# Loading the query weights as fifteen strided 16-row transfers, one of them ahead of the first keys

## The chip, the cores and the metric

The kernel runs on one core of a Trainium2 chip. A time is the device time of one execution in microseconds (us); the median of several executions is quoted.

## The reference, cut to what matters

One decode step: four batch entries, one token each, width 512. The token is normalised, multiplied by the query weights `wq` (512 x 4096), scored against 1024 cached keys for 8 key heads, and the result goes through `wo`; an MLP gate runs beside it.

```python
xn = layernorm(x)
q  = (xn @ wq).reshape(B, 1, 32, 128)          # wq: 512 x 4096 bf16, 4 MB
p  = softmax(q @ K[:, :, -1024:] / sqrt(128))  # K: 8 MB read
s  = (p @ V[:, :, -1024:]) @ wo                # V: 8 MB, wo: 4 MB
g  = silu(mlp(layernorm(xn)))                  # w1, w2: 3.7 MB
out = x + s * g
```

The kernel reads 28.85 MB and does little arithmetic on it.

## The kernel before

All large loads are issued by SyncE (SP), one after the other, and run on the core's 16 DMA engines. The order is K0, K1, wq in two halves, K2 to K7, then V (with the two MLP weights behind V0 and V1) and `wo`. Row `4p + c` of `wq` goes to partition `p`, slot `c`, so each partition's 32 KB are contiguous in memory.

```python
    def load_k(g):
        d_k[g] = pg.dma("sp", "k%d" % g, lambda e: e.dma_start(
            kv_buf[:, g, :, :].rearrange("p c d -> p (c d)"), cache_rows(A_k_cache, g)))
    # ... (cut)
    load_k(0)
    load_k(1)
    wq_r = A_wq.rearrange("(p c) n -> p c n", c=4)
    d_wq = [pg.dma("sp", "wq%d" % c, lambda e, c=c: e.dma_start(
        wq_sb[:, 2 * c:2 * c + 2, :], wq_r[:, 2 * c:2 * c + 2, :])) for c in range(2)]
    for g in range(2, HKV):
        load_k(g)
    # ... (cut) the query product waits for the two halves of wq in turn
    add("pe", lambda pe: f_q(pe, 0), v_xT, d_wq[0])
    t_q = add("pe", lambda pe: f_q(pe, 1), d_wq[1])
```

The softmax here doesn't subtract the row's maximum and nothing guards it: scores larger than these inputs give would overflow.

## Time and profile before

| | before |
|---|---|
| time, median | 77.41 us (77.17 to 78.25, 3 runs) |
| span of the profile | 75.4 us |
| first bytes of the large stream | 2.20 us |
| stream rate between 5 and 70 us | about 424 GB/s |
| 16 KB packet, median | 611 ns |
| last landing of `wq` | 19.5 us |
| end of the stream (last landing of `wo`) | 72.25 us |

A descriptor is one row's copy order. A "packet" is one copy's record in the trace; a "landing" is one rise of the semaphore of a transfer after its issue: a K transfer has 16 of them, the 4-row x transfer 4. Both are counted in the trace one by one; it doesn't say which DMA engine one belongs to. The strip, the windows, the chain and the queue's timeline of this kernel are shown and read in the prediction below.

One line more, from the timeline of the last matmuls: start, length, what, and in brackets the idle time ahead of it and what ended that.

```profile
68.61 3.42 PE L486 MATMUL psM<-OW,wo_sb 128*128 128x4 bf16 x120 [0.51 <-DVE OW L472]
72.29 0.37 PE L486 MATMUL psM<-OW,wo_sb 128*128 128x4 bf16 x8 [0.26 <-DMA wo_sb<-in_A_wo_dram]
```

The last eight matmuls waited 0.26 us for the end of the stream.

### The profile page before, as it was taken

The page shows a single profiled execution, that of the slowest core. Times are in us where ns is not written, and L with a number is a line of the kernel's source. Part 1 is how long each engine was busy: PE and PEld are TensorE (multiplying, and loading weights), DVE is VectorE, ACT ScalarE, POOL GpSimd, SP SyncE. Part 2 cuts the span into 40 slices and gives each one's busy share as a digit, 9 for nine tenths or more (in the row PEclk, how much of TensorE's full clock was granted, in tenths as well). Part 3 has the DMA queues.
Part 4 walks back from the last instruction along what each step waited for, and adds up shares of the span by engine and source line. Part 5 has one row for each costly group of instructions (what it writes and reads, how often), then busy time and mean ns, then how long its engine had stood idle before and what let it go on. Part 6 is the DMA issues. An engine that isn't in the chain of part 4 may idle for free.

```text
span 75.4 us, 2408 instructions
## 1 busy us (share of the span) xinstructions
PE 54.1 (72%) x1107; PEld 46.0 (61%) x1107; DVE 38.0 (50%) x84; ACT 9.0 (12%) x16; POOL 4.5 (6%) x13
## 2 busy tenths in 40 slices
PE   0009992500659999999999945999759989937950
PEld 0009871200228999999999935999459766806930
DVE  0878996000033599999999000000891678781010
ACT  0611000000054031231131520000200000000000
POOL 6970000000000000000000000000000000000000
PEclk9999999955555799999999997555555555555555
DMA  0899999999999999999999999999999999999600
GB/s 2 280 413 439 454 426 417 434 434 382 434 421 421 421 430 430 443 413 437 451 389 439 440 412 396 426 430 426 434 417 421 419 411 424 417 408 412 255 13 2
DMA packets 4213, 28.99 MB, mean 384 GB/s; under 512 B 486, under 2 KB 491, under 8 KB 1644
## 3 DMA queue, kind: packets, MB, share of 16 engines
q1 hardware_dynamic: 4160, 28.84, 91.7%
q8 instruction: 8, 0.13, 0.6%
q10 hardware_dynamic: 44, 0.01, 0.1%
q14 instruction: 1, 0.01, 0.0%
HBM read 28.85 MB, written 0.00 MB: 382 GB/s over the span
## 4 chain that ended last, share of the span: by engine, by line
DMA 46%; PE 29%; SPq 20%; DVE 2%; issue 1%
DMA wo_sb<-in_A_wo_dram 24%; DMA wq_sb<-in_A_wq_dram 22%; SPq L454 17%; PE psK L279 16%; PE psS L298 6%; PE psO L362 3%; PE psS L294 2%; SPq L207 2%; PE psK L374 1%; DVE q_sb L368 1%; SPq L219 1%; PE psS L516 1%; PE psM L486 1%; SPq L212 0%; DVE o_bf L518 0%
## 5 line engine op out<-in xcount | busy, mean ns | idle before, releaser
L279 PE MATMUL psK<-ident,kv_buf 128*128 128x128 bf16 x256 | 21.0, 234 | 5.7 <-DMA kv_buf<-in_A_k_cache_dram 5.7
L285 DVE COPY kt_buf<-psK 128x1024 bf16<-128x1024 bf16 x32 | 20.7, 686 | 2.2 <-PE psK L279 2.2
L279 PEld LDWEIGHTS psK<-ident,kv_buf 128*128 128x128 bf16 x256 | 16.5, 105 | 6.3 <-DMA kv_buf<-in_A_k_cache_dram 5.7
L298 PE MATMUL psS<-qT,kt_buf 128*128 128x16 bf16 x256 | 10.3, 170 | 0.0
L298 PEld LDWEIGHTS psS<-qT,kt_buf 128*128 128x128 bf16 x256 | 9.6, 97 | 1.1 <-issue 0.3
L316 PEld LDWEIGHTS psO<-P_buf,kv_buf 128*128 128x128 bf16 x256 | 7.7, 103 | 2.2 <-issue 1.9
L316 PE MATMUL psO<-P_buf,kv_buf 128*128 128x16 bf16 x256 | 8.2, 174 | 0.3
L392 PE MATMUL psM<-yT,w_sb 128*128 128x4 bf16 x56 | 5.7, 204 | 1.8 <-issue 1.8
L362 PE MATMUL psO<-wq_sb,xT 128*32 128x512 bf16 x32 | 2.9, 503 | 5.6 <-DMA wq_sb<-in_A_wq_dram 5.6
L306 ACT ACTIVATE P_buf<-psS 128x512 bf16<-128x512 f32 x8 | 4.8, 598 | 15.6 <-PE psS L298 15.6
L329 DVE TENSOR_REDUCE den_sb<-psS 128x16 f32<-128x512 f32 x8 | 5.5, 689 | 1.7 <-PE psS L322 1.4
L400 DVE TENSOR_SCALAR t_sb<-u_sb 128x56 f32<-128x56 f32 x1 | 0.2, 192 | 11.4 <-ACT u_sb L399 11.4
L392 PEld LDWEIGHTS psM<-yT,w_sb 128*128 128x128 bf16 x56 | 4.5, 153 | 2.2 <-issue 2.1
L362 PEld LDWEIGHTS psO<-wq_sb,xT 128*32 128x32 bf16 x32 | 0.8, 112 | 6.9 <-DMA wq_sb<-in_A_wq_dram 5.7
L368 DVE CAST q_sb<-psO 128x512 bf16<-128x512 f32 x1 | 0.7, 691 | 8.4 <-PE psO L362 8.4
L322 PE MATMUL psS<-P_buf,ones_bf 128*128 128x512 bf16 x8 | 4.5, 561 | 0.0
L486 PE MATMUL psM<-OW,wo_sb 128*128 128x4 bf16 x128 | 3.8, 166 | 0.8 <-DVE OW L472 0.5
L486 PEld LDWEIGHTS psM<-OW,wo_sb 128*128 128x128 bf16 x128 | 3.6, 104 | 0.9 <-issue 0.6
L294 PE MATMUL psS<-negm,ind 128*128 128x512 bf16 x8 | 3.3, 410 | 0.0
L419 PE MATMUL psM<-hT,w_sb 128*128 128x4 bf16 x56 | 2.1, 167 | 1.4 <-DVE hT L411 1.4
L394 PE MATMUL psM<-ones_bf,b_sb 1*128 1x4 bf16 x14 | 3.0, 215 | 0.0
L419 PEld LDWEIGHTS psM<-hT,w_sb 128*128 128x128 bf16 x56 | 1.8, 105 | 1.9 <-DVE hT L411 1.9
(63 smaller groups left out, 28.9 us busy)
## 6 DMA issues: line engine op xcount, KB each, us to landing
kv_buf<-in_A_k_cache_dram SPq DMA_DIRECT2D x8, 1024.0 KB, 21.3
kv_buf<-in_A_v_cache_dram SPq DMA_DIRECT2D x8, 1024.0 KB, 22.6
wq_sb<-in_A_wq_dram SPq DMA_DIRECT2D x2, 2048.0 KB, 13.9
w_sb<-in_B_w_dram SPq DMA_DIRECT2D x2, 1792.0 KB, 31.2
wo_sb<-in_A_wo_dram SPq DMA_DIRECT2D x3, 1024.0 KB, 24.8
wo_sb<-in_A_wo_dram SPq DMA_DIRECT2D x1, 512.0 KB, 21.4
wo_sb<-in_A_wo_dram SPq DMA_DIRECT2D x2, 256.0 KB, 17.8
x<-in_A_x_dram ACTq DMA_DIRECT2D x2, 2.0 KB
```

Source lines behind the costliest of these rows:

```text
L279: last = pe.transpose(psK[n % NB][:, j * 128:(j + 1) * 128], kv_buf[:, g, u * UT + j, :], ident[:, :])
L285: cp[n] = add("dve", lambda e: e.tensor_copy(kt_buf[:, n % NKT, :], psK[n % NB][:, 0:1024]), t, sc.get(n - NKT))
L294: pe.matmul(psS[g % 2][:, 0:512], ind[:, :], negm[:, :], start=True, stop=False, skip_group_check=True)
L298: last = pe.matmul(psS[g % 2][:, c * 16:(c + 1) * 16], kt_buf[:, n % NKT, j * 128:(j + 1) * 128], qT[:, g * 16:(g + 1) * 16], start=False, ...
L306: ex[g] = add("act", lambda e: e.activation(P_buf[:, g, :], psS[g % 2][:, 0:512], AF.Exp, scale=SCALE), sc[n])
L316: last = pe.matmul(pso[:, 0:16], kv_buf[:, (HKV + g) % NS, c, :], P_buf[:, g, c * 16:(c + 1) * 16], start=(c == 0), stop=(c == NC - 1))
L322: den[g] = add("pe", lambda pe: pe.matmul(psS[g % 2][:, 0:512], ones_bf[:, :], P_buf[:, g, :], start=True, stop=True), ex[HKV - 2 + g % 2] ...
L329: v = add("dve", lambda e: e.tensor_reduce(den_sb[:, cs], bass.AP(psS[g % 2], 0, [[512, 128], [1, 16], [16, NC]]), AX.X, ALU.add), den[g])
L362: last = pe.matmul(psO[m // 4][32 * s:32 * s + 32, 0:512], xT[:, c, :], wq_sb[:, c, m * 512:(m + 1) * 512], start=(c == 0), stop=(c == 3), ...
L392: pe.matmul(o, bass.AP(w1_sb, c * F + k, [[4 * F, 128], [FC, 128]]), yT[:, c * 4:(c + 1) * 4], start=(c == 0), stop=False)
L454: e.dma_start(wo_sb[:, g0:g1, i0:i1, :], wo_r[:, g0:g1, i0:i1, :]))))
L486: last = pe.matmul(psM[:, PS_W + c * 4:PS_W + (c + 1) * 4], wo_sb[:, g, i, c * 128:(c + 1) * 128], OW[:, i, g * 4:(g + 1) * 4], start=firs ...
```

## The change

Its intent: let the first transfer have few descriptors, so that all 16 DMA engines get work sooner, and keep the partitions of the following ones in the same pattern. The group `s` of a transfer is every eighth partition, `s, 8+s, ..., 120+s`: sixteen rows.

```diff
+    wq_r = A_wq.rearrange("(q s c) n -> s q (c n)", s=8, c=4)
+    wq_v = wq_sb[:, :, :].rearrange("p c n -> p (c n)")
+    d_wq = [[pg.dma("sp", "wqa", lambda e: e.dma_start(wq_v[0:128:8, :], wq_r[0, :, :]))], []]
     load_k(0)
     load_k(1)
-    wq_r = A_wq.rearrange("(p c) n -> p c n", c=4)
-    d_wq = [pg.dma("sp", "wq%d" % c, lambda e, c=c: e.dma_start(
-        wq_sb[:, 2 * c:2 * c + 2, :], wq_r[:, 2 * c:2 * c + 2, :])) for c in range(2)]
+    for c in range(2):
+        for s in range(1, 8):
+            n = HQ * DH * 2
+            d_wq[c].append(pg.dma("sp", "wq%d_%d" % (c, s), lambda e, n=n, c=c, s=s: e.dma_start(
+                wq_v[s:128:8, c * n:(c + 1) * n], wq_r[s, :, c * n:(c + 1) * n])))
@@ (cut) the query product @@
-    add("pe", lambda pe: f_q(pe, 0), v_xT, d_wq[0])
-    t_q = add("pe", lambda pe: f_q(pe, 1), d_wq[1])
+    add("pe", lambda pe: f_q(pe, 0), v_xT, *d_wq[0])
+    t_q = add("pe", lambda pe: f_q(pe, 1), *d_wq[1])
```

## The prediction

Passages are cut from the text below, each marked. Two terms of the sum are +9.7 us and -1.0 us, the author's estimate: the packets of wq take twice as long as the 611 ns measured (16 x 0.611 = 9.8 us becomes 19.5), and about 1 us of that comes back where the group changes. The two sums: 85.8 us with these terms, 77.1 us without. Rivals: R1 (no loss, 77.1 us) and R2 (the loss shrinks to one group of three or four transfers, about 2 us: 79 us); the chances given were 0.60 for a doubling, 0.10 for a partial loss (R2, R3) and 0.30 for none.

> **What bounds the kernel now.** I read the strip of forty slices first, then the table of windows, then the chain of waits, then the DMA queue's own timeline. The strip (busy tenths of each engine, then the DMA's share and rate) says which resource never rests:
>
> ```profile
> PE   0009992500659999999999945999759989937950
> DVE  0878996000033599999999000000891678781010
> DMA  0899999999999999999999999999999999999600
> GB/s 2 280 413 439 454 426 417 434 434 382 434 421 421 421 430 430 443 413 437 451 389 439 440 412 396 426 430 426 434 417 421 419 411 424 417 408 412 255 13 2
> ```
>
> PE and DVE have holes; the DMA row stands at 9 from the third slice to the thirty-seventh. The windows (length, busy time of PE, PEld, DVE, ACT and POOL, granted clock, DMA share, GB/s) give the rate:
>
> ```profile
> 5.00:10.00 5.00, 4.26 (x48) 3.94 (x48) 4.59 (x12) 0.20 (x1) 0.34 (x1) 1.00 1.04 429
> 10.00:15.00 5.00, 2.74 (x42) 1.62 (x40) 2.63 (x6) 0.00 (x0) 0.00 (x0) 1.00 1.02 436
> ...
> 55.00:60.00 5.00, 4.47 (x125) 4.07 (x126) 2.73 (x9) 0.18 (x1) 0.00 (x0) 0.50 1.00 419
> ...
> 70.00:71.00 1.00, 1.00 (x44) 1.00 (x41) 0.00 (x0) 0.00 (x0) 0.00 (x0) 0.50 0.71 272
> 71.00:72.00 1.00, 1.00 (x36) 0.94 (x33) 0.00 (x0) 0.00 (x0) 0.00 (x0) 0.50 0.36 139
> ```
>
> So this is one stream of 28.85 MB at about 424 GB/s. 28.85 MB / 424 GB/s is 68.0 us; it starts a little after 2 us and its last bytes land at 72.25. The packets say the same per engine: 8 KB took 309 ns and 16 KB 611 ns, nearly always, which is 26.5 GB/s an engine, times 16 is 424. All 16 engines run flat out, so only three things can move the time: an earlier start of the stream, a lower rate in it, or a longer tail.
>
> The chain of waits (start, length, what) names other pieces, and must be read with that in mind:
>
> ```profile
> 2.78 16.73 DMA wq_sb<-in_A_wq_dram
> ...
> 41.55 0.60 SPq L454
> ...
> 54.36 17.89 DMA wo_sb<-in_A_wo_dram
> ```
>
> It goes through the query weights (landing at 19.5 us), the score phase and the output-weight issues. But while PE waited for wq the stream moved 410 to 436 GB/s of other data. Bringing wq in earlier therefore buys nothing by itself; wq's place matters only through the bytes of the stream. After 72.25 there are 3.2 us of tail (last eight matmuls, two DVE operations, output DMA), and the measured time stands 2.0 us above the profiled span (77.41 against 75.4). The change touches neither.
>
> The queue's timeline (start, length, line, issue) shows the beginning that the change aims at:
>
> ```profile
> 0.81 1.26 SPq L207 DMA_DIRECT2D kv_buf<-in_A_k_cache_dram  x2
> 2.12 1.17 SPq L219 DMA_DIRECT2D wq_sb<-in_A_wq_dram  x2
> 3.33 3.84 SPq L207 DMA_DIRECT2D kv_buf<-in_A_k_cache_dram  x6
> ```
>
> A 128-row transfer costs SP about 0.6 us to issue; the first K bytes move in the window from 2.00 to 2.25 us.
>
> [...]
>
> **The change, part by part.**
>
> *Removed:* two wq transfers of 128 descriptors of 16 KB, 1.17 us of SP issue. *Added:* one transfer of 16 descriptors of 32 KB, and fourteen of 16 descriptors of 16 KB. The bytes are equal: 4 MB, 256 KB an engine, 9.6 us of stream.
>
> *Issue.* The output DMA, also 16 rows, took SP 0.36 us. Fifteen of those are 5.4 us against 1.17, 4.2 us more of SP. Does SP starve the stream? Each small transfer carries 256 KB, 0.62 us of stream, for about 0.40 us of issue with its gap, and 2.5 MB (6 us) stand queued ahead of them. K2 is issued near 8 us instead of 3.3, V0 near 12 instead of 9.0; by then over 3 MB are queued. No cost.
>
> *Semaphore packets.* 13 transfers more, one 9 ns packet per engine each (the trace's 4-byte packets): 0.12 us on the stream.
>
> *Start.* The x transfer, issued at 0.80, moved its first bytes in the window from 1.50 to 1.75; K0, issued at 0.81 with 128 rows, in that from 2.00 to 2.25. A 16-row first transfer should follow x: about 0.45 us earlier. Its 32 KB an engine last at least 1.2 us, long enough for K0's descriptors to be there. Gain about 0.45 us, all of it on the path.
>
> [...]
>
> [...] 77.4 - 0.45 + 0.12 + 9.7 - 1.0 = 85.8 us. [...] 77.4 - 0.45 + 0.12 = 77.1 us.
>
> Would a wq that lands near 29 us instead of 19.5 bring another bound? V2 was issued at 26.96 after the scores began. 18.4 MB stood ahead of it in the stream, enough to about 45 us, so an issue near 36 us still comes in time. PE's work after the scores stays behind the stream as before.
>
> **The rivals.** [...] *R3: small transfers are paced by SP.* Each would need over 0.62 us of issue; 0.36 us speaks against it. It would cost under 3 us. *R4: the start gain is larger than I take it.* The stream can't begin before SP's first issue at 0.81 plus x's 0.8 us, so nothing beyond 0.7 us.
>
> **Range and chances.** [...] Over 2% faster means 1.55 us gained, three times what the earlier start offers: 0.03. Within 2%: 0.31. Slower by over 2%: 0.66. The predicted time lies in the larger heap, 85.4 us; an honest 8-in-10 range has to reach into the other: 76.8 to 87.0.
>
> **What would show it.** [...] between about 6 and 26 us the rate is 210 to 300 GB/s instead of 424, the DMA share stays near 1, and 16 KB packets of wq take about 1.2 us instead of 0.611; wq's last landing moves to 27 to 29 us; the end of the stream moves to about 81 us. [...] The start: first stream bytes at about 1.75 us. Issue: small transfers at 0.3 to 0.4 us on SP, no low DMA share between them. [...]

## The result, and the profile after

| | before | after |
|---|---|---|
| time, median | 77.45 us (6 runs) | 86.92 us (86.77 to 87.5, 6 runs) |
| span of the profile | 75.4 us | 85.1 us |
| first bytes of the stream | 2.20 us | 2.20 us |
| 16 KB packets of `wq`, median | 611 ns | 1253 ns |
| last landing of `wq` | 19.5 us | 27.9 us |
| end of the stream | 72.25 us | 81.94 us |

The ratio is 1.1216, 95% interval 1.1157 to 1.1274: 12% slower. (A ratio here is the mean time of one kernel's fast runs over that of the other's in the same rounds, so it isn't quite the ratio of the medians quoted.)

The strip of the changed kernel, the same two rows as before:

```profile
DMA  0999999999998999999999999999999999999810
GB/s 2 256 301 425 409 216 246 185 216 216 246 193 192 427 423 431 416 427 423 416 447 428 401 439 439 407 415 423 420 427 431 427 410 416 423 410 418 326 49 2
```

A slice is now 2.1 us. The DMA row is as full as before, but from the sixth slice to the thirteenth the engines move 185 to 246 GB/s. They are busy with half the bytes. The windows (columns as before; the last three are granted clock, DMA share and GB/s) date it:

```profile
5.00:8.00 3.00, 0.00 (x0) 0.00 (x0) 2.20 (x7) 0.20 (x1) 0.34 (x1) 1.00 0.96 394
10.00:25.00 15.00, 6.04 (x73) 4.20 (x71) 4.70 (x9) 0.00 (x0) 0.00 (x0) 0.78 1.02 220
```

(The view counts a packet whole in the window in which it starts. So a share can read above 1, and a short window can read far above 424 GB/s.) While K0 and K1 pass, the rate is 394; while the fourteen wq transfers pass, it is 220 at a DMA share of 1.02. The engines show a full busy share at half the usual 424 GB/s, since a 16 KB packet takes 1253 ns instead of 611; that is the sign to look for here. The queue's timeline (start, length, line, issue):

```profile
0.80 0.62 SPq L220 DMA_DIRECT2D wq_sb<-in_A_wq_dram  x1
1.48 1.26 SPq L207 DMA_DIRECT2D kv_buf<-in_A_k_cache_dram  x2
2.78 8.97 SPq L226 DMA_DIRECT2D wq_sb<-in_A_wq_dram  x14
11.80 3.83 SPq L207 DMA_DIRECT2D kv_buf<-in_A_k_cache_dram  x6
```

The opening transfer has 16 rows and still took SP 0.62 us, as a K transfer does; the fourteen took 0.64 us each with their gaps. The chain of waits still names wq, and is of as little help as before:

```profile
11.17 16.77 DMA wq_sb<-in_A_wq_dram
...
66.64 15.30 DMA wo_sb<-in_A_wo_dram
```

Where the 9.7 us of span went can be read from landings. K1's last landing moved from 8.41 to 11.07 us, 2.66 us later; 1.24 us of that is the opening transfer's own 512 KB at 424 GB/s, now ahead of K1, so 1.42 us is loss. From there to the last landing of wq it took 16.87 us for 3.67 MB; at the kernel before's pace (15 of its 16 landings had come by 18.11 us, from 8.41, for 4.19 MB) that would be 8.5 us: 8.4 us of loss. Together 9.8 us, against 9.69 us by which the end of the stream moved. That leaves nothing of size for the rest of the kernel.

### The profile page after: what moved, and what is told of

Its sections match the earlier page's. It is cut to its first block, busy times and chain, and to the rows that moved or that the text cites. A ratio compares the mean times of both kernels' runs of the same rounds, so it can differ in the third digit from the quotient of the medians.

```text
span 85.1 us, 2415 instructions
## 1 busy us (share of the span) xinstructions
PE 54.0 (63%) x1095; PEld 47.1 (55%) x1107; DVE 38.5 (45%) x84; ACT 9.0 (11%) x16; POOL 4.5 (5%) x13
## 4 chain that ended last, share of the span: by engine, by line
DMA 38%; SPq 30%; PE 26%; issue 2%; DVE 1%
DMA wq_sb<-in_A_wq_dram 20%; SPq L461 18%; DMA wo_sb<-in_A_wo_dram 18%; PE psK L286 15%; SPq L226 9%; PE psS L305 6%; PE psO L369 2%; SPq L207 1%; PE psK L381 1%; DVE q_sb L375 1%; SPq L220 1%; PE psS L523 0%; PE psM L493 0%; SPq L212 0%; DVE o_bf L525 0%
## 5 line engine op out<-in xcount | busy, mean ns | idle before, releaser
L286 PE MATMUL psK<-ident,kv_buf 128*128 128x128 bf16 x256 | 21.6, 239 | 8.2 <-DMA kv_buf<-in_A_k_cache_dram 8.2
L286 PEld LDWEIGHTS psK<-ident,kv_buf 128*128 128x128 bf16 x256 | 17.2, 108 | 8.5 <-DMA kv_buf<-in_A_k_cache_dram 8.2
L369 PE MATMUL psO<-wq_sb,xT 128*32 128x512 bf16 x32 | 3.8, 625 | 10.9 <-DMA wq_sb<-in_A_wq_dram 10.9
L376 ACT ACTIVATE q_sb<-psO 128x512 bf16<-128x512 f32 x1 | 0.6, 597 | 23.2 <-PE psO L369 23.2
```

What stands on the lines that cost most here:

```text
L286: last = pe.transpose(psK[n % NB][:, j * 128:(j + 1) * 128], kv_buf[:, g, u * UT + j, :], ident[:, :])
L369: last = pe.matmul(psO[m // 4][32 * s:32 * s + 32, 0:512], xT[:, c, :], wq_sb[:, c, m * 512:(m + 1) * 512], start=(c == 0), stop=(c == 3), ...
```

## The experiments

**Theories.** *Placement:* which partitions a transfer writes sets how long its packets take, twice as long for every eighth partition. *Source pitch:* the sixteen source rows are 256 KB apart, and the memory is read more slowly. *One descriptor:* a transfer of so few rows that each landing stands for one packet is slow by itself. *Opening:* putting a wq transfer first is what costs. The expectations below are cut where they give the reason for the placement theory; numbers right after such a mark, with no theory and no condition named, are that theory's.

### Four ways to place the sixteen rows

Each is the changed kernel with other partitions or other source rows. All four gave right results.

**Sixteen neighbours.**

```diff
-    wq_r = A_wq.rearrange("(q s c) n -> s q (c n)", s=8, c=4)
+    wq_r = A_wq.rearrange("(s q c) n -> s q (c n)", s=8, c=4)
-    ... wq_v[0:128:8, :] ...    wq_v[s:128:8, ...]
+    ... wq_v[0:16, :] ...       wq_v[16 * s:16 * s + 16, ...]
```

> Same fifteen transfers of 16 rows, but each to sixteen neighbouring partitions (16s to 16s+15) from sixteen neighbouring rows of wq (32 KB apart instead of 256 KB). Right result. [...] 16 KB packets near 2.4 us (four times 0.611), the wq part at 105 to 150 GB/s, time 97 to 106 us. Source-pitch theory (HBM slowed by rows 256 KB apart): packets back at 0.61 us, 77 us. Theory that a transfer of one descriptor per engine is slow by itself: as the changed kernel, 87 us, packets 1.25 us.

Measured: 101.57 us (one run). 208 of 224 packets of 16 KB took 2.0 to 2.3 us, median 2.16. Two windows of it:

```profile
15.00:20.00 5.00, 0.86 (x16) 0.60 (x13) 1.80 (x5) 0.00 (x0) 0.00 (x0) 1.00 1.04 125
25.00:30.00 5.00, 1.82 (x16) 0.53 (x16) 0.00 (x0) 0.00 (x0) 0.00 (x0) 0.50 1.02 121
```

The number and size of the transfers and of their packets are those of the changed kernel, and the source pitch is eight times smaller; the rate fell to 121 to 125 GB/s, a little above a quarter of 424. Only the placement theory expected that. (Why it was 2.16 rather than 2.44 us was not shown.)

This run shows one thing more. Its opening transfer also has 16 rows, but SP issued it in 0.38 us, and the first bytes came at 1.81 us:

```profile
0.80 0.38 SPq L220 DMA_DIRECT2D wq_sb<-in_A_wq_dram  x1
```

So in this one run the earlier start that the change was after is there with sixteen neighbouring partitions; with every eighth it is not.

**Same partitions, neighbouring source rows.** The normalised x is written in the matching order, so the product is right.

```diff
-    wq_r = A_wq.rearrange("(q s c) n -> s q (c n)", s=8, c=4)
+    wq_r = A_wq.rearrange("(s q c) n -> s q (c n)", s=8, c=4)
-    v_xn = add("dve", lambda e: e.tensor_copy(xn_bf[:, :], xn32[:, :]), v)
+    v_xn = add("dve", lambda e: e.tensor_copy(
+        bass.AP(xn_bf, 0, [[512, 4], [4, 8], [32, 16], [1, 4]]),
+        bass.AP(xn32, 0, [[512, 4], [64, 8], [4, 16], [1, 4]])), v)
```

> Destinations as in the changed kernel (every eighth partition), but the sixteen source rows of a transfer are neighbours (32 KB apart); the normalised x is permuted to match, so the result is right. [...] nothing changes, 86 to 88 us, 16 KB packets 1.25 us. Source-pitch theory: packets 0.61 us, 77 us. One-descriptor theory: 87 us.

Measured: 88.2 us (one run), packets 1.25 us in the median, 213 GB/s in the windows from 15 to 25 us. The source pitch is not the cause. The run stands 0.2 us above the range given: one of K1's sixteen landings came 2.1 us after the other fifteen, before the wq part, and one was 1.3 to 1.7 us behind through nearly all of it. That was not pursued. (The opening took SP 0.62 us here too, so it is not the source rows that make its issue long.)

**Every seventh partition.**

```diff
-    ... wq_v[0:128:8, :], wq_r[0, :, :]
+    ... wq_v[0:112:7, :], wq_r[0:112:7, :]          # wq_r: "(p c) n -> p (c n)"
-    ... wq_v[s:128:8, ...], wq_r[s, :, ...]
+    ... wq_v[slice(s, 112, 7) if s < 7 else slice(112, 128), ...], and the same rows of wq_r
```

> Every seventh partition (seven groups over partitions 0 to 111) and partitions 112 to 127 as the eighth group; still 16 rows a transfer, one descriptor per engine, right result. [...] of the 192 packets of 16 KB in stride-7 groups at least 150 at 0.61 us and at most 40 near 1.2 us, 32 packets of the last group near 2.4 us; time 79 to 85 us. One-descriptor theory: all near 1.25 us, 87 us. Source-pitch theory (224 KB, no power of two): all 0.61 us, 77 us.

Measured: 86.19 us (one run), 1.2 us above the range. The packets contradict every theory as stated: 3 of 224 were below 0.70 us, 163 took 0.70 to 1.10. From one transfer's landings to the next it took 0.80 to 0.84 us on average in the groups from partitions 3 and 4, and 0.97 to 1.09 us in those from 1, 2 and 5 (the groups next to the last one, of sixteen neighbours, are mixed with it). So far more packets were slow than the at most 40 that the placement theory gave to these groups. This was taken up again below.

**Thirty-two rows, every fourth partition.**

```diff
-    wq_r = A_wq.rearrange("(q s c) n -> s q (c n)", s=8, c=4)
+    wq_r = A_wq.rearrange("(q s c) n -> s q (c n)", s=4, c=4)
-    for s in range(1, 8):       # ... wq_v[s:128:8, ...]
+    for s in range(1, 4):       # ... wq_v[s:128:4, ...]; opening: wq_v[0:128:4, :]
```

> Every fourth partition, 32 rows a transfer, two descriptors per engine: one opening transfer of 1 MB and six of 512 KB. [...] 77 us with packets of 0.611 us [...]; 83 to 87 us [...]. Source-pitch theory: 128 KB or 256 KB apart, 80 to 87 us. One-descriptor theory: half of the loss, 82 us. Early start: none gained, since the first issue took 0.62 us with 16 rows too.

Measured: 77.33 us, ratio to before 1.0012 (0.9979 to 1.0046). 191 of 192 packets of 16 KB took 611 ns. Windows of it:

```profile
10.00:15.00 5.00, 4.66 (x53) 4.49 (x50) 4.30 (x7) 0.00 (x0) 0.00 (x0) 1.00 1.03 439
15.00:20.00 5.00, 2.52 (x40) 1.06 (x40) 1.38 (x5) 0.45 (x1) 0.00 (x0) 1.00 0.98 416
```

Small transfers, a stride over partitions and a wq transfer ahead of K are all still there; the loss is gone. Of the two times that the placement theory left open, 77 us and 83 to 87 us, it is the first.

### The patterns by themselves, the opening, and halves

**Test patterns.** The kernel before, with groups of four transfers put ahead of everything, each group behind a full transfer and alone on the queues. Each group's row length differs, which labels its packets.

```diff
+    for k, s in enumerate(PAT):                      # s: slice of partitions
+        w = 8192 - 128 * (k + 1)
+        now = [dma(wo_flat[:, 0:8192] <- src[:, 0:8192], after the group before)]
+        for j in range(4):
+            now.append(dma(kv_flat[s, 8192 * j:8192 * j + w] <- src[s, 0:w]))
```

> The kernel before with twelve groups of four test transfers ahead of everything; each group stands behind one full 128-row transfer and waits for the group before, so each pattern is alone on the queues. Rows of 16 KB less 256 bytes times the group's number, which labels the packets. Result right, time far longer on purpose (200 to 300 us); only packet durations are read, as a multiple of the undisturbed one (bytes / 27.25 plus 9 ns, from the kernel before). [...] every 8th partition 2.0; 0..15 4.0; every 7th from 3 1.0 for 14 of 16 rows and 2.0 for two; 0..63 2.0; 32..95 1.0; 32 rows every 4th 1.0; 16 rows every 4th (0..60) 2.0; 0..31 2.0; 8 rows every 4th from 0 (0..28) 1.0; the same from 4 (4..32) 1.0; 8 rows every 8th (0..56) 2.0; 8 rows every 16th 2.0. [...] Rival: one descriptor per transfer is slow: then 0..28, 4..32 and every 7th all near 2.0.

Measured (243.58 us, one run, result right): median packet time over the undisturbed one.

| partitions | expected | measured median |
|---|---|---|
| every 8th, 16 rows | 2.0 | 2.05 |
| 0..15 | 4.0 | 3.94 |
| every 7th from 3 | 1.0 (two rows 2.0) | 1.06 (up to 2.1) |
| 0..63, 64 rows | 2.0 | 2.10 |
| 32..95, 64 rows | 1.0 | 1.00 |
| every 4th, 32 rows | 1.0 | 1.00 |
| 0, 4, .., 60 | 2.0 | 2.08 |
| 0..31 | 2.0 | 2.09 |
| 0, 4, .., 28 (8 rows) | 1.0 | 1.00 |
| 4, 8, .., 32 (8 rows) | 1.0 | 1.00 |
| every 8th, 0..56 (8 rows) | 2.0 | 2.05 |
| every 16th (8 rows) | 2.0 | 2.04 |

All twelve medians agree with the expected numbers within 6%. The rows 0..63 and 32..95 are the plainest pair: equal counts and sizes; partitions 32..63 are in both, and 0..31 in the one stand against 64..95 in the other. (Source rows move with the partitions in these patterns. That they are not the cause rests on the run with neighbouring source rows.) Two windows inside these two groups, in this order:

```profile
52.00:66.00 14.00, 0.00 (x0) 0.00 (x0) 0.00 (x0) 0.00 (x0) 0.00 (x0) 1.00 1.01 207
76.00:84.00 8.00, 0.00 (x0) 0.00 (x0) 0.00 (x0) 0.00 (x0) 0.00 (x0) 1.00 1.01 421
```

The two groups of 8 rows from 0 and from 4, with half the descriptors of a 16-row transfer and at 1.00, rule out the one-descriptor theory.

**Halves of 64 neighbours**, in the kernel before; no small transfers, no opening.

```diff
-    d_wq = [dma(wq_sb[:, 2*c:2*c+2, :] <- wq_r[:, 2*c:2*c+2, :]) for c in range(2)]
+    d_wq = [[dma(wq_sb[64*h:64*h+64, 2*c:2*c+2, :] <- wq_r[64*h:64*h+64, 2*c:2*c+2, :])
+             for h in range(2)] for c in range(2)]
```

> The kernel before with each wq transfer cut into its two halves of 64 neighbouring partitions: four transfers, 64 descriptors of 16 KB each, no early start, no small transfers. [...] packets of 1.2 us, 85 to 88 us. Small-transfer theories: 77 to 78 us.

Measured: 87.53 us (one run), packets 1.275 us in the median. A window:

```profile
15.00:20.00 5.00, 0.93 (x12) 0.47 (x16) 0.00 (x0) 0.00 (x0) 0.00 (x0) 0.70 1.01 213
```

Nothing of the change is in this kernel but that a transfer writes only some of the partitions, and it loses about what the change loses (one run).

**The opening undone**, once without and once with the loss in the wq part: K0 and K1 are issued ahead of the first wq transfer.

```diff
+    load_k(0)
+    load_k(1)
     d_wq = [[dma(wqa)], []]
-    load_k(0)
-    load_k(1)
```

> The 32-row version with K0 and K1 ahead of the first wq transfer: [...]. If the opening gains nothing (first bytes came at 2.15 to 2.20 us with either), 77.3 us and a ratio to before within 0.5%; had it gained the predicted 0.45 us it would be 77.8 against 77.3.

> The changed kernel with its opening transfer put behind K1: fifteen small transfers, no opening. [...] the loss stays, 86.5 to 87.5 us, [...]. If the opening itself were what costs: 77 to 80 us.

Measured: 77.19 us, ratio 0.9954 (0.9926 to 0.9982) for the 32-row version, and 86.96 us, ratio 1.1204 (1.1167 to 1.1241) for the changed kernel. Neither needs the opening, and neither is hurt by it. The 0.5% of the first is not a gain of the placement that I would build on: the kernel before itself moved between 77.12 and 77.74 us on the two chips of these experiments, and the two 32-row versions ran on different chips.

### An early start without the cost of the placement

In the test-pattern run, SP issued a flat transfer of 128 rows of 16 KB in 0.33 to 0.40 us. Two more kernels use that form: as a control, in the old order, and as an opening ahead of K0.

```diff
+    wq_r = A_wq.rearrange("(p c) n -> p (c n)", c=4)
+    d_wq = [dma(wq_v[:, 0:8192] <- wq_r[:, 0:8192])]          # flat_open; flat_mid: after K1
     load_k(0)
     load_k(1)
+    d_wq.append(dma(wq_v[:, 8192:16384] <- wq_r[:, 8192:16384]))
```

> Control: the kernel before, same transfers in the same order, only written as a flat two-dimensional pattern (128 rows of 16 KB), whose issue took SP 0.33 to 0.40 us in the test-pattern run instead of 0.58. Nothing before wq is touched: ratio to before within 0.3%, 77.4 us.

> The change's aim without its cost: the first half of wq as one flat 128-row transfer ahead of K0 and K1, the second half after them. If the start of the stream hangs on how long the first issue takes, first bytes move from 2.2 to about 1.85 us (0.40 us issue instead of 0.63) and the time falls by about 0.35 us: ratio 0.995, 77.1 us. If the start is fixed by something else, first bytes stay at 2.2 us and the ratio is 1.00.

Measured: the control 77.93 us, ratio 1.0031 (0.9981 to 1.0081), with single runs from 77.46 to 78.38 beside 77.2 to 78.07 of the kernel before; its two flat transfers behind K1 took SP 1.09 us instead of 1.17, so the short issue was not found behind other transfers. The flat opening 77.44 us, ratio 0.9976 (0.9932 to 1.002). The stream did start earlier, as these two lines of the flat opening show (issue; a window with its GB/s last):

```profile
0.80 0.39 SPq L220 DMA_DIRECT2D wq_sb<-in_A_wq_dram  x1
```

```profile
1.75:2.00 0.25, 0.00 (x0) 0.00 (x0) 0.00 (x0) 0.08 (x1) 0.25 (x2) 1.00 2.62 541
```

In the kernel before, that quarter microsecond moved 12 GB/s. First bytes came at 1.83 us instead of 2.20. But the first megabyte was complete at 5.32 us against 5.23 before, and the stream ended at 72.21 against 72.25: the lead was gone within the first 3 us. The first descriptors of the stream are slow in both kernels (8 KB took about 600 ns instead of 309 in the kernel before; in the window above, 541 GB/s at a share of 2.62 is 206 GB/s for a full share); why is open. And even a lead that lasts would have met PE:

```profile
69.36 3.69 PE L491 MATMUL psM<-OW,wo_sb 128*128 128x4 bf16 x128 [0.51 <-DVE OW L477]
```

Here all 128 last matmuls ran without a wait for the stream; PE had become the end. Part of that is this kernel's own doing: with 2 MB of wq ahead, K0 landed at 10.63 us instead of 5.70, and PE started on it later. So this run could not have shown the gain in its time, and that the lead was lost is read from the stream alone. In the kernel before, the 0.26 us of slack was all that an earlier stream could have won. In the 32-row version the last matmuls waited 1.48, 0.29 and 0.21 us, so there PE was not in the way, and the start gained nothing because the first bytes (2.15 us) hardly came earlier.

### Why so many packets slowed in the stride-7 run

Two readings are in this expectation. The first (the numbers up to "mixed groups") is that only some packets of a transfer take 2.0; its rival (1.1 to 1.7) is that the others are slowed too. For the last group: 2.0 or less, down to 1.0.

> Seven groups of four test transfers, [...] every 7th partition from 0, from 1, from 2, from 4 (each four times), then 1,2,3,4 in a row, then 3,4,3,4, then every 8th from 0,4,0,4. [...] 4 of 16 packets at 2.0 in the first three groups, 2 of 16 in the fourth, the rest 1.0, also in the mixed groups. [...] median of all packets 1.1 to 1.7, [...]. [...] Time far longer on purpose; result right.

The edit changes only the list of patterns in the test-pattern kernel. Measured (158.03 us, one run, result right):

| partitions | packets of 16 expected at 2.0 | measured median | packets below 1.15, of 64 |
|---|---|---|---|
| every 7th from 0 | 4 | 1.98 | 16 |
| every 7th from 1 | 4 | 1.99 | 16 |
| every 7th from 2 | 4 | 2.03 | 16 |
| every 7th from 4 | 2 | 1.04 | 58 |
| from 1, 2, 3, 4 in a row | 4, 4, 2, 2 | 1.42 | 14 |
| from 3, 4, 3, 4 | 2 | 1.24 | 22 |
| every 8th from 0, 4, 0, 4 | 16 or fewer | 1.73 | 12 |

From 4, four times over, 58 of 64 packets run free. From 0, 1 and 2 all but the first sixteen packets slow, to a median of 2.0, and not only 4 of each 16. Where 3 and 4 alternate, most packets are slow as well (22 of 64 below 1.15), although neither is by itself (1.06 and 1.04). The rival, that the other packets are slowed too, is right, but its size (1.1 to 1.7) was not: 2.0 from 0, 1 and 2, 1.04 from 4. What links the packets isn't in the trace and stays open. The last row answers another point: alternating between every 8th from 0 and from 4 gives back some of the loss (1.73 against 2.05); why is open too.

## Why the prediction was right

**The bound** was read rightly: the stream sets the end before and after, and a loss in its rate came through in full (9.8 us of loss read from the landings, 9.69 us at the end of the stream).

**The rate of the wq part**, +9.7 us, was the step that carried the prediction, and the runs show it: packets of 1253 ns where 1.2 us were named, wq's last landing at 27.9 us where 27 to 29 were named, the end of the stream at 81.94 where about 81 was. That the choice of partitions does it is shown by neighbours (121 to 125 GB/s, little over a quarter of 424), by the 32-row version (77.33 us, no loss), by halves of 64 rows (87.53 us, the same loss without the change) and by the twelve patterns. What it is in the hardware that makes one choice slower than another was not shown. Before the runs the term was the author's estimate, since the trace before could not show it; the kernel before had no large partial transfer.

**The start**, a gain of 0.45 us, did not come. It was read from the x transfer, which has 4 rows, and the step assumed that issue time follows the number of rows. The 16-row opening took SP 0.62 us, and the first bytes came at 2.20 us as before. With sixteen neighbouring partitions it took 0.38 us and the first bytes came at 1.81, so what counted was which partitions, not how many rows. The flat opening then showed that a real lead of 0.37 us is lost in the first megabyte, and that PE had come close enough to cover part of it.

**The 1.0 us given back** where the group changes was there, but came to less and was eaten up. From one transfer's landings to the next it took 1.17 us on average next to a change between the groups 1 to 3 and 4 to 7 and in the last transfer (seven transfers), and 1.27 elsewhere (seven): about 0.65 us back. But 1.27 is more than twice 0.611, as the test patterns' 2.05 to 2.10 are, and that cost about 0.6 us over the fourteen. Net, the end of the stream moved by 9.69 us, the whole of the loss. The loss didn't shrink after the first groups (1.27 us early and late), so rival R2 fell. These two terms, 0.45 and 1.0, are why the sum read 85.8 and the kernel 86.9. (The prediction then states 85.4 without saying what the other 0.4 is.)

**Luck.** The range, 76.8 to 87.0 us, reached over both outcomes, loss or no loss, so a time inside it proves little; and the median stands 0.08 us below its upper end, with two of the six runs (87.05 and 87.5) above it. What speaks for the prediction is that the signs of the wq part were named beforehand and found; those of the start and of the issue were not.

**The issue**, 0.36 us a transfer from the output DMA (whose sixteen partitions are neighbours), was 0.64. The conclusion, no cost, held, since the DMA share stayed near 1. But it held because the packets were slow: 3.67 MB in 8.97 us is 409 GB/s, a little less than the 424 that the stream takes with packets of 611 ns. In a form with such packets, R3 might have been close (not run).

**R1**, no loss, fell with the packet times. The semaphore packets (0.12 us) are too small to be seen. A reading to put right: the time stands 1.8 us above the span of the same execution (77.16 against 75.4), not 2.0; it is the same before and after.

## What to carry to other kernels

Before cutting a transfer by partitions, compare each piece with the patterns measured here. Packets ran at 1.00 for partitions 32..95, for every fourth of 128, and for 8 rows at 0, 4, .., 28; they took 2.04 to 2.10 for every eighth, every sixteenth, 0..63, 0..31 and 0, 4, .., 60, and 3.94 for sixteen neighbours. A pattern not in the tables is worth a test transfer first: every seventh took from 1.04 to 2.03 by where it began. A busy DMA at half its rate (a share of 1.02 at 220 GB/s) was the mark of having got it wrong, and since one stream bound the kernel, the loss arrived in full. An earlier first issue is worth little if, as here, the first descriptors are slow and another engine is a quarter of a microsecond behind the stream.
